# A two-stage FFT filter and gated feed-forward kernel: the operands of its f32r matmuls at other byte offsets

## The chip, the cores and the metric

The kernel runs on one core of a Trainium2 chip. The metric is the device time of one execution in microseconds, from its start to its end. "Before" has a median of 1559.99 us over 2 runs (1559.17 to 1560.82). A core has a matrix engine (TensorE; PE in the profile, and PEld for its weight loads), a vector engine (VectorE, DVE), a scalar engine (ScalarE, ACT), GpSimd (POOL) and DMA queues, of which SP issues most. Engines work on SBUF, 128 partitions with a run of bytes each, and TensorE writes its sums to PSUM. An *offset* in this document is where a tile's or a slice's first byte lies within its partition; only its remainder after division by 256 is spoken of.

## The reference

Eight batches of 3136 rows of 256 values are filtered along the rows in the frequency domain, and the result goes through a gated feed-forward layer of width 1024 whose gate is a three-tap convolution along the rows:

```python
X = np.fft.rfft(x, axis=1)
Y = X * (filt_r + 1j * filt_i)[None, :, :]
y = np.fft.irfft(Y, n=x.shape[1], axis=1).astype(np.float32)
h = np.maximum(y @ w_in, 0.0)                     # 3136 x 1024 per batch
hp = pad(h, 1 row of zeros at both ends)
conv_out = sum(conv_w[k] * hp[:, k:k + S, :] for k in range(3))
gate = 1.0 / (1.0 + np.exp(-conv_out))
out = (h * gate @ w_out).astype(np.float32)
```

## The kernel before

**Stage one** (up to about 360 us) does the filter. Each batch goes through 14 pieces: a first transform (`first`, L323), transposes (`turn`, L334), a second transform (`second`, L346 and L349), the product with the filter on VectorE and GpSimd (`filt`), and a third transform (`third`, L233), whose result is stored to `b_dram`. Its matmuls are plain float32, and each takes two passes over its columns in the trace (the transposes one). Beside it, `convert_weights` turns the 64-bit weights into float32 and splits each into a high and a low part of type f32r: `hi_act` (ScalarE, L146) writes the high part, rounded to f32r, and `lo_pool` (GpSimd, L152) the difference. These are the tiles `wi` (`w_in`: 2 halves of the contraction, k, by 1024 columns) and `wo` (`w_out`: 8 slices f by 256 columns).

**Stage two** is the feed-forward layer. The order of the work is written out by hand in the loop over m at the end: 28 chunks j of 896 rows, by 8 slices f of 128 hidden units, by 2 halves i of 448 rows. In each step TensorE does three things.

- `inner` (L456) makes a 128 x 450 block of hidden values from `wi` and the filtered rows `y`. Since both are split in two, a product is three matmuls, high by high, high by low and low by high (`mm3`, L177, L178, L179), for each of the two halves k: six matmuls of 450 columns, with a slice of `wi` as the stationary operand (the weights that are loaded) and 450 columns of `y` as the moving one.
- `project` (L488) multiplies the gated values `g` of an earlier step (6 steps behind, PLAG) with `wo`: three matmuls again for each block of 128 rows (L498 to L500), nine or twelve in a step, with `g` stationary and 256 columns of `wo` moving.
- in some steps `last_stage` (L215) does a part of the last transform of a later batch, from rows `br` that SP loads from `b_dram` (`last_load`, L198); `last_out` splits its result into `y` high (L146) and `y` low (L149).

ScalarE and VectorE work on the hidden block between: ReLU (L465), the three taps (L467, L472, L473), the sigmoid (L477), the product (L478); `split_g` then writes `g` high (ScalarE, L146) and `g` low (GpSimd, L152).

TensorE loads the weights of the next matmul while the moving rows of the present one stream in, so it reads two places of SBUF at once. Where tiles lie is set by the pools: `wc` holds `wi` and `wo` for the whole run, `y_even` and `y_odd` hold `y` of even and odd batches, `wp` holds four pairs of `g` in turn. The tiles' sizes therefore fix every offset:

```python
wi = [wc.tile([128, KT, FF], F32R, name=f"wi{h}") for h in range(2)]          # L189
wo = [wc.tile([128, NF, D], F32R, name=f"wo{h}") for h in range(2)]           # L190
ys[b] = [yps[b % 2].tile([128, KT, S + 2], F32R, name=f"y{h}") for h in range(2)]   # L203
gs[j, f] = [wp.tile([128, 2 * SUB], F32R, name=f"g{h}", bufs=4) for h in range(2)]  # L483
```

In the built program these come out, modulo 256 bytes, as follows: every slice of `wi` and `wo`, high and low, at 160; `g`, high and low, at 224; `y` high at 160 and `y` low at 192 in its first half (k = 0), 168 and 200 in its second, for each of the seven sub-blocks of 448 rows (1792 bytes, a multiple of 256) and in both pools.

Of the kernel before, what the change touches and what calls it, by code (L numbers as in the profile page):

```python
# [10 lines left out]
F32R = mybir.dt.float32r  # L11
# [5 lines left out]
S = 3136  # L17
# [3 lines left out]
D = 256  # L21
FF = 1024
KT = D // 128
NF = FF // 128
SUB = 448
# [99 lines left out]
def tile_fft_filter_gated_ffn(  # L125
# [16 lines left out]
    nc = tc.nc  # L142
    B = x.shape[0]

    def hi_act(dst, src):
        nc.scalar.activation(dst, src, AF.Copy)  # L146
# [4 lines left out]
    def lo_pool(dst, src, hi):  # L151
        nc.gpsimd.tensor_tensor(out=dst, in0=src, in1=hi.bitcast(F32), op=ALU.subtract)  # L152

    def to_f32(dst, raw, e, m):


        v = nc.vector
        pairs = raw.rearrange("p (n t) -> p n t", t=2)
        low, high = pairs[:, :, 0].bitcast(U32), pairs[:, :, 1]
        v.tensor_scalar(e, high, 3, 0x3FFFFFF8, op0=ALU.logical_shift_left, op1=ALU.bitwise_and)  # L160
        yield
        v.tensor_scalar(m, high, 30, 30, op0=ALU.logical_shift_right, op1=ALU.logical_shift_left)
        yield
        v.tensor_tensor(out=e, in0=e, in1=m, op=ALU.bitwise_or)
        yield
        v.tensor_scalar(m, high, 27, 0xF, op0=ALU.logical_shift_right, op1=ALU.bitwise_and)
        yield
        v.scalar_tensor_tensor(out=dst, in0=m, scalar=7.0, in1=e.bitcast(F32), op0=ALU.is_ge, op1=ALU.mult)
        yield
        v.tensor_scalar(e, dst.bitcast(I32), 23, 23, op0=ALU.logical_shift_right, op1=ALU.logical_shift_left)  # L170
        yield
        v.scalar_tensor_tensor(out=e.bitcast(F32), in0=low, scalar=2.0**-52, in1=e.bitcast(F32), op0=ALU.mult, op1=ALU.mult)
        yield
        nc.gpsimd.tensor_tensor(out=dst, in0=dst, in1=e.bitcast(F32), op=ALU.add)

    def mm3(ps, wh, wl, rh, rl, start=True, stop=True, **kw):
        nc.tensor.matmul(ps, lhsT=wh, rhs=rh, start=start, stop=False, **kw)  # L177
        nc.tensor.matmul(ps, lhsT=wh, rhs=rl, start=False, stop=False, **kw)  # L178
        nc.tensor.matmul(ps, lhsT=wl, rhs=rh, start=False, stop=stop, **kw)  # L179
# [4 lines left out]
    wc = ctx.enter_context(tc.tile_pool(name="wc", bufs=1))  # L184
# [1 line left out]
    cw = wc.tile([128, 3, NF], F32, name="cw")  # L186
    nc.gpsimd.memset(cw[:, 0, 0:1], 0.0)
    nc.scalar.activation(cw[:, 0, 0:1], cw[:, 0, 0:1], AF.Sigmoid)
    wi = [wc.tile([128, KT, FF], F32R, name=f"wi{h}") for h in range(2)]  # L189
    wo = [wc.tile([128, NF, D], F32R, name=f"wo{h}") for h in range(2)]  # L190


    ys, yps = {}, []
# [6 lines left out]

    def y_slices(b, sl):
        if sl.start == 0:
            ys[b] = [yps[b % 2].tile([128, KT, S + 2], F32R, name=f"y{h}") for h in range(2)]  # L203
            for t in ys[b]:
                nc.gpsimd.memset(t[:, :, 0:1].bitcast(F32), 0.0)
                nc.gpsimd.memset(t[:, :, S + 1:S + 2].bitcast(F32), 0.0)
        return (t[:, :, 1:S + 1].rearrange("p k (a c) -> p k c a", c=N2)[:, :, sl] for t in ys[b])
# [10 lines left out]
    def last_out(b, c):  # L218
        yh, yl = y_slices(b, slice(c, c + 2))
        pv = lasts.pop((b, c))[:, 0:4 * N1].rearrange("p (k c a) -> p k c a", c=2, a=N1)  # L220
        hi_act(yh, pv)
        lo_dve(yl, pv, yh)
# [5 lines left out]
    parts = {}  # L228
# [16 lines left out]
    with (  # L245
# [36 lines left out]
        def load_weights(k):  # L282
            raws[k] = raw = cv.tile([128, 2, 512], I32, name="raw")
            for part, src in enumerate((w_in, w_out)):
                nc.sync.dma_start(out=raw[:, part], in_=src[:, 512 * k:512 * k + 512])
# [6 lines left out]
        def convert_weights():  # L292

            for k in range(8):
                raw = raws.pop(k)
                em = cv.tile([128, 2, 512], I32, name="em", bufs=1)
                ws = cv.tile([128, 2, 256], F32, name="ws")
                yield from to_f32(ws.rearrange("p t n -> p (t n)"), raw.rearrange("p t n -> p (t n)"), em[:, 0], em[:, 1])
                yield
                parts = [[t.rearrange("p a b -> p (a b)")[:, 256 * k:256 * k + 256] for t in w] for w in (wi, wo)]  # L300
                for part, (wh, wl) in enumerate(parts):
                    hi_act(wh, ws[:, part])
                yield
                for part, (wh, wl) in enumerate(parts):
                    lo_pool(wl, ws[:, part], wh)
                yield
                if k < 6:
                    load_weights(k + 2)
# [130 lines left out]
    wp = ctx.enter_context(tc.tile_pool(name="wp", bufs=2, reuse_waits="tile"))  # L439
# [4 lines left out]
    hs, ts, gs, pos = {}, {}, {}, {}  # L444
# [8 lines left out]

    def inner(j, f, i):
        ps = ps_h.tile([128, 512], F32, name="ps_h")[:, 0:SUB + 2]
        fs = slice(128 * f, 128 * f + 128)  # L456
        b, u = divmod(2 * j + i, NSUB)
        us = slice(u * SUB, u * SUB + SUB + 2)
        for k in range(KT):
            mm3(ps, wi[0][:, k, fs], wi[1][:, k, fs], ys[b][0][:, k, us], ys[b][1][:, k, us], start=k == 0, stop=k == KT - 1)  # L460
        hs[j, f, i] = ps

    def relu(j, f, i):
# [16 lines left out]
    def split_g(j, f, i):  # L480
        t = ts.pop((j, f, i))
        if i == 0:
            gs[j, f] = [wp.tile([128, 2 * SUB], F32R, name=f"g{h}", bufs=4) for h in range(2)]  # L483
        gh, gl = (g[:, i * SUB:i * SUB + SUB] for g in gs[j, f])
        hi_act(gh, t)
        lo_pool(gl, t, gh)

    def project(j, f, i):  # L488
        gh, gl = gs[j, f]
        if f == 0 and i == 0:  # L490
            pos[j] = [ps_o.tile([128, 512], F32, name=f"po{k}") for k in range(4)], wp.tile([128, NT, D], F32, name="ot")
        po, ot = pos[j]
        tiles = range(4) if i == 0 else range(4, NT)
        for t in tiles:
            o = po[t // 2][:, t % 2 * D:t % 2 * D + D]
            sl = slice(128 * t, 128 * t + 128)
            first, last = f == 0 and t % 2 == 0, f == NF - 1
            nc.tensor.matmul(o, lhsT=gh[:, sl], rhs=wo[0][:, f], start=first, stop=False, skip_group_check=True)  # L498
            nc.tensor.matmul(o, lhsT=gh[:, sl], rhs=wo[1][:, f], start=False, stop=False, skip_group_check=True)  # L499
            nc.tensor.matmul(o, lhsT=gl[:, sl], rhs=wo[0][:, f], start=False, stop=last, skip_group_check=True)  # L500

    def evacuate(j, f, i):
        if f < NF - 1:
# [17 lines left out]
    for b in range(1, B):  # L521
        start = ((NSUB * (b - 1) - 1) // 2 + 1) * 16 + (4 if b == 1 else 0)
        stop = NSUB * b // 2 * 16 + NSUB * b % 2
# [73 lines left out]
```

## Time and profile before

| what | us |
|---|---|
| median of 2 runs | 1559.99 |
| the profiled execution's own time | 1559.94 |
| its span in the profile | 1558.2 |
| TensorE matmuls busy | 1537.8 |
| TensorE weight loads busy | 1418.2 |
| VectorE busy | 1297.0 |
| ScalarE busy | 1245.0 |
| GpSimd busy | 703.0 |

The span is the time between the first and the last recorded instruction; the 1.7 us between it and the execution's time lie around it. Busy time of an engine is the time in which at least one of its instructions was running. A matmul's recorded duration includes its way through the array, and the next starts before it ends; how fast matmuls follow each other is read from their starts. The profile's chain of waits goes back from the last instruction to whatever released each; its shares say which work the end hung on.

### The profile page before, as it was taken

Reading aid. Unit: us, or ns where it says so; the run is one execution under the profiler, and the core shown is the slowest. Engines: PE = TensorE matmul, PEld = TensorE weight load, DVE = VectorE, ACT = ScalarE, POOL = GpSimd, SP = SyncE. Lnnn points to the kernel's source line nnn. Section 1 sums busy time; section 2 is a strip of 40 time slices with the busy share of each in tenths; the row PEclk is TensorE's granted clock in tenths of the full one; section 3 lists DMA queues with packets and bytes.
Section 4 is the critical chain, followed back from the end, with each engine's and each line's share of the span. In section 5 each row is a group of like instructions: output and inputs, shape, how many; then the busy total and the mean of one; then the engine's idle time right before and its main releaser. Section 6 shows DMA issues by size and latency. Waiting matters only on the chain.

```text
span 1558.2 us, 27801 instructions
## 1 busy us (share of the span) xinstructions
PE 1537.8 (99%) x10320; PEld 1418.2 (91%) x10320; DVE 1297.0 (83%) x1978; ACT 1245.0 (80%) x2274; POOL 703.0 (45%) x625
## 2 busy tenths in 40 slices
PE   8999999998999999999999999999999999999998
PEld 7787778877999999999999999999999999999998
DVE  3888888788888888888888888888888888888887
ACT  5655555566888888888888888888888888888887
POOL 3455555533444444444444444444444434444444
PEclk9999999999999999999999999999999999999999
DMA  9855555452111011111111011111011110100001
GB/s 236 261 179 168 172 169 164 137 148 78 33 52 48 31 47 48 49 49 47 48 42 36 27 53 52 44 48 48 31 48 42 49 54 27 46 25 25 24 25 48
DMA packets 89062, 115.24 MB, mean 74 GB/s; under 512 B 7400, under 2 KB 60168, under 8 KB 88928
## 3 DMA queue, kind: packets, MB, share of 16 engines
q1 hardware_dynamic: 74592, 87.77, 18.4%
q10 hardware_dynamic: 14336, 25.70, 5.8%
q8 instruction: 82, 1.34, 0.4%
q14 instruction: 52, 0.43, 0.1%
HBM read 62.06 MB, written 51.38 MB: 73 GB/s over the span
## 4 chain that ended last, share of the span: by engine, by line
PE 94%; DMA 2%; DVE 1%; ACT 1%; issue 0%; SPq 0%; POOL 0%; ACTq 0%; POOLq 0%; DVEq 0%
PE ps_h L178 12%; PE ps_h L179 12%; PE ps_h L177 11%; PE po L498 11%; PE po L500 11%; PE po L499 11%; PE ps L233 6%; PE ps_h L215 5%; PE pp L346 5%; PE ps L323 5%; PE ps L334 3%; DMA x<-in_x 1%; PE ps L215 1%; DVE y L149 1%; ACT y L146 0%; PE pp L349 0%
## 5 line engine op out<-in xcount | busy, mean ns | idle before, releaser
L152 POOL TENSOR_TENSOR g<-t,g 128x448 fp32r<-128x448 f32 x448 | 517.1, 1154 | 663.5 <-ACT g L146 259.3
L498 PE MATMUL po<-wo,g 128*128 128x256 f32 x1568 | 441.4, 282 | 0.0
L500 PE MATMUL po<-wo,g 128*128 128x256 f32 x1568 | 433.9, 277 | 0.4 <-POOL g L152 0.4
L499 PE MATMUL po<-wo,g 128*128 128x256 f32 x1568 | 433.4, 276 | 0.0
L472 DVE SCALAR_TENSOR_TENSOR t<-ps_h,cw,t 128x448 f32<-128x448 f32 x448 | 305.7, 682 | 85.6 <-ACT t L467 75.2
L178 PE MATMUL ps_h<-y,wi 128*128 128x450 f32 x896 | 330.3, 369 | 5.6 <-DVE y L149 5.6
L177 PE MATMUL ps_h<-y,wi 128*128 128x450 f32 x896 | 329.1, 367 | 3.3 <-DVE t L478 1.9
L179 PE MATMUL ps_h<-y,wi 128*128 128x450 f32 x896 | 328.8, 367 | 0.0
L473 DVE SCALAR_TENSOR_TENSOR t<-ps_h,cw,t 128x448 f32<-128x448 f32 x448 | 306.5, 684 | 16.0
L467 ACT ACTIVATE t<-ps_h,cw 128x448 f32<-128x448 f32 x448 | 284.8, 636 | 43.2 <-ACT ps_h L465 2.6
L498 PEld LDWEIGHTS po<-wo,g 128*128 128x128 f32 x1568 | 294.8, 188 | 7.1
L499 PEld LDWEIGHTS po<-wo,g 128*128 128x128 f32 x1568 | 294.3, 188 | 5.7
L500 PEld LDWEIGHTS po<-wo,g 128*128 128x128 f32 x1568 | 294.5, 188 | 0.6 <-POOL g L152 0.6
L465 ACT ACTIVATE ps_h<-ps_h 128x450 f32<-128x450 f32 x448 | 251.8, 562 | 32.9 <-PE ps_h L179 27.0
L478 DVE TENSOR_TENSOR t<-ps_h,t 128x448 f32<-128x448 f32 x448 | 275.3, 615 | 0.1
L477 ACT ACTIVATE t<-t 128x448 f32<-128x448 f32 x448 | 255.0, 569 | 12.4 <-DVE t L473 11.2
L146 ACT ACTIVATE g<-t 128x448 fp32r<-128x448 f32 x448 | 254.7, 568 | 0.2 <-DVE t L478 0.2
L362 POOL TENSOR_TENSOR z<-u,v 120x512 f32<-120x512 f32 x112 | 156.6, 1398 | 184.3 <-DVE v L360 154.1
L178 PEld LDWEIGHTS ps_h<-y,wi 128*128 128x128 f32 x896 | 168.3, 188 | 14.7 <-DVE y L149 7.9
L179 PEld LDWEIGHTS ps_h<-y,wi 128*128 128x128 f32 x896 | 168.3, 188 | 13.9
L177 PEld LDWEIGHTS ps_h<-y,wi 128*128 128x128 f32 x896 | 169.9, 190 | 11.7 <-DVE t L478 2.9
L149 DVE TENSOR_TENSOR y<-ps_h,y 128x448 fp32r<-128x448 f32 x98 | 103.1, 1053 | 75.3 <-ACT y L146 75.3
(62 smaller groups left out, 1661.6 us busy)
## 6 DMA issues: line engine op xcount, KB each, us to landing
x<-in_x SPq DMA_DIRECT2D x112, 224.0 KB, 2.9
b_dram<-sb ACTq DMA_DIRECT2D x112, 224.0 KB, 2.3
br<-b_dram SPq DMA_DIRECT2D x112, 224.0 KB, 2.6
out<-ot SPq DMA_DIRECT2D x27, 896.0 KB, 4.1
raw<-in_w_in SPq DMA_DIRECT2D x8, 256.0 KB
raw<-in_w_out SPq DMA_DIRECT2D x8, 256.0 KB
t_sb<-in_fr SPq DMA_DIRECT2D x15, 112.0 KB
t_sb<-in_fi SPq DMA_DIRECT2D x14, 112.0 KB
```

What stands on the lines that cost most here:

```text
L152: nc.gpsimd.tensor_tensor(out=dst, in0=src, in1=hi.bitcast(F32), op=ALU.subtract)
L177: nc.tensor.matmul(ps, lhsT=wh, rhs=rh, start=start, stop=False, **kw)
L178: nc.tensor.matmul(ps, lhsT=wh, rhs=rl, start=False, stop=False, **kw)
L179: nc.tensor.matmul(ps, lhsT=wl, rhs=rh, start=False, stop=stop, **kw)
L467: nc.scalar.activation(t, h[:, 1:SUB + 1], AF.Copy, scale=cw[:, 1, f:f + 1])
L472: nc.vector.scalar_tensor_tensor(out=t, in0=h[:, 0:SUB], scalar=cw[:, 0, f:f + 1], in1=t, op0=ALU.mult, op1=ALU.add)
L473: nc.vector.scalar_tensor_tensor(out=t, in0=h[:, 2:SUB + 2], scalar=cw[:, 2, f:f + 1], in1=t, op0=ALU.mult, op1=ALU.add)
L477: nc.scalar.activation(t, t, AF.Sigmoid)
L478: nc.vector.tensor_mul(t, h[:, 1:SUB + 1], t)
L498: nc.tensor.matmul(o, lhsT=gh[:, sl], rhs=wo[0][:, f], start=first, stop=False, skip_group_check=True)
L499: nc.tensor.matmul(o, lhsT=gh[:, sl], rhs=wo[1][:, f], start=False, stop=False, skip_group_check=True)
L500: nc.tensor.matmul(o, lhsT=gl[:, sl], rhs=wo[0][:, f], start=False, stop=last, skip_group_check=True)
```

## The change

The tiles get larger, and their parts are taken from other places in them; what is computed, and in which order on the compute engines, stays.

- `wi` has, for each half k and slice f, 136 columns of room of which 128 are used, so that slice f starts 32 bytes further (modulo 256) than slice f - 1. `wo` has 264 columns of room for each slice, of which 256 are used: 32 bytes further per slice too. The conversion of the weights writes and reads the same values in that layout; for `wi` its 256 elements are now two pieces of 128.
- `y` has S + 64 columns of room, a multiple of 256 bytes for each half, and batch b starts 8 b columns, 32 b bytes, into it.
- `g` has 64 columns more, and chunk j starts 8 (j mod 8) columns, 32 (j mod 8) bytes, into it.

All tiles of a pair now have sizes that are multiples of 256 bytes, so that high and low parts start at equal offsets: in the built program `wi` and `wo` at 160 + 32 f, `y` at 160 + 32 b (odd batches) or 224 + 32 b (even ones) in both halves, `g` at 160 + 32 (j mod 8).

```diff
@@ -186,8 +186,8 @@
     cw = wc.tile([128, 3, NF], F32, name="cw")
     nc.gpsimd.memset(cw[:, 0, 0:1], 0.0)
     nc.scalar.activation(cw[:, 0, 0:1], cw[:, 0, 0:1], AF.Sigmoid)
-    wi = [wc.tile([128, KT, FF], F32R, name=f"wi{h}") for h in range(2)]
-    wo = [wc.tile([128, NF, D], F32R, name=f"wo{h}") for h in range(2)]
+    wi = [wc.tile([128, KT, NF, 136], F32R, name=f"wi{h}") for h in range(2)]
+    wo = [wc.tile([128, NF, D + 8], F32R, name=f"wo{h}") for h in range(2)]
 
 
     ys, yps = {}, []
@@ -200,7 +200,8 @@
 
     def y_slices(b, sl):
         if sl.start == 0:
-            ys[b] = [yps[b % 2].tile([128, KT, S + 2], F32R, name=f"y{h}") for h in range(2)]
+            ys[b] = [yps[b % 2].tile([128, KT, S + 64], F32R, name=f"y{h}") for h in range(2)]
+            ys[b] = [t[:, :, 8 * b:8 * b + S + 2] for t in ys[b]]
             for t in ys[b]:
                 nc.gpsimd.memset(t[:, :, 0:1].bitcast(F32), 0.0)
                 nc.gpsimd.memset(t[:, :, S + 1:S + 2].bitcast(F32), 0.0)
@@ -297,12 +298,14 @@
                 ws = cv.tile([128, 2, 256], F32, name="ws")
                 yield from to_f32(ws.rearrange("p t n -> p (t n)"), raw.rearrange("p t n -> p (t n)"), em[:, 0], em[:, 1])
                 yield
-                parts = [[t.rearrange("p a b -> p (a b)")[:, 256 * k:256 * k + 256] for t in w] for w in (wi, wo)]
-                for part, (wh, wl) in enumerate(parts):
-                    hi_act(wh, ws[:, part])
+                f = k % 4 * 2
+                parts = [[t[:, k // 4, f:f + 2, 0:128] for t in wi], [t[:, k, 0:D] for t in wo]]
+                values = [ws[:, 0].rearrange("p (f n) -> p f n", f=2), ws[:, 1]]
+                for (wh, wl), v in zip(parts, values):
+                    hi_act(wh, v)
                 yield
-                for part, (wh, wl) in enumerate(parts):
-                    lo_pool(wl, ws[:, part], wh)
+                for (wh, wl), v in zip(parts, values):
+                    lo_pool(wl, v, wh)
                 yield
                 if k < 6:
                     load_weights(k + 2)
@@ -453,11 +456,10 @@
 
     def inner(j, f, i):
         ps = ps_h.tile([128, 512], F32, name="ps_h")[:, 0:SUB + 2]
-        fs = slice(128 * f, 128 * f + 128)
         b, u = divmod(2 * j + i, NSUB)
         us = slice(u * SUB, u * SUB + SUB + 2)
         for k in range(KT):
-            mm3(ps, wi[0][:, k, fs], wi[1][:, k, fs], ys[b][0][:, k, us], ys[b][1][:, k, us], start=k == 0, stop=k == KT - 1)
+            mm3(ps, wi[0][:, k, f, 0:128], wi[1][:, k, f, 0:128], ys[b][0][:, k, us], ys[b][1][:, k, us], start=k == 0, stop=k == KT - 1)
         hs[j, f, i] = ps
 
     def relu(j, f, i):
@@ -480,7 +482,8 @@
     def split_g(j, f, i):
         t = ts.pop((j, f, i))
         if i == 0:
-            gs[j, f] = [wp.tile([128, 2 * SUB], F32R, name=f"g{h}", bufs=4) for h in range(2)]
+            gs[j, f] = [wp.tile([128, 2 * SUB + 64], F32R, name=f"g{h}", bufs=4) for h in range(2)]
+            gs[j, f] = [g[:, j % 8 * 8:j % 8 * 8 + 2 * SUB] for g in gs[j, f]]
         gh, gl = (g[:, i * SUB:i * SUB + SUB] for g in gs[j, f])
         hi_act(gh, t)
         lo_pool(gl, t, gh)
@@ -495,9 +498,9 @@
             o = po[t // 2][:, t % 2 * D:t % 2 * D + D]
             sl = slice(128 * t, 128 * t + 128)
             first, last = f == 0 and t % 2 == 0, f == NF - 1
-            nc.tensor.matmul(o, lhsT=gh[:, sl], rhs=wo[0][:, f], start=first, stop=False, skip_group_check=True)
-            nc.tensor.matmul(o, lhsT=gh[:, sl], rhs=wo[1][:, f], start=False, stop=False, skip_group_check=True)
-            nc.tensor.matmul(o, lhsT=gl[:, sl], rhs=wo[0][:, f], start=False, stop=last, skip_group_check=True)
+            nc.tensor.matmul(o, lhsT=gh[:, sl], rhs=wo[0][:, f, 0:D], start=first, stop=False, skip_group_check=True)
+            nc.tensor.matmul(o, lhsT=gh[:, sl], rhs=wo[1][:, f, 0:D], start=False, stop=False, skip_group_check=True)
+            nc.tensor.matmul(o, lhsT=gl[:, sl], rhs=wo[0][:, f, 0:D], start=False, stop=last, skip_group_check=True)
 
     def evacuate(j, f, i):
         if f < NF - 1:
```

On SP's queue two of the first four loads of `br` wait for more than before, since the pool `lp` now begins 960 bytes lower and its buffers lie on other tiles of stage one (`Pool_49`, `DVE_49` and `PE_49` are the counters of those engines, the `DMAHW` ones those of DMA queues). Before, where stage one's last loads of `x` end and stage two's first loads of `br` begin:

```order
L314 DMA x<-in_x 112x512 [waits DMAHW5_49,PE_49]
L198 DMA br<-b_dram_57 112x2x256 [waits DMAHW5_49,Pool_49]
L198 DMA br<-b_dram_57 112x2x256 [waits DMAHW6_49,PE_49]
L198 DMA br<-b_dram_57 112x2x256 [waits DMAHW0_49]
L198 DMA br<-b_dram_57 112x2x256 [waits DMAHW1_49]
```

The same place after, with the lines of the changed file:

```order
L317 DMA x<-in_x 112x512 [waits DMAHW5_49,PE_49]
L198 DMA br<-b_dram_57 112x2x256 [waits DMAHW5_49,DMAHW6_49,DVE_49,Pool_49]
L198 DMA br<-b_dram_57 112x2x256 [waits DMAHW6_49,PE_49]
L198 DMA br<-b_dram_57 112x2x256 [waits DMAHW0_49,Pool_49]
L198 DMA br<-b_dram_57 112x2x256 [waits DMAHW1_49]
```

No load moved; the first waits for VectorE and another DMA queue too, the third for GpSimd.

## The prediction

> **What bounds the kernel now.** I read the page first, for the engine that the span belongs to; then the table by windows, for the stage in which the change acts; then the groups by line, for the two kinds of matmul that the change touches; and last the timeline, for how far apart these matmuls start, which their durations do not tell.
>
> ```profile
> span 1558.2 us, 27801 instructions
> PE 1537.8 (99%) x10320; PEld 1418.2 (91%) x10320; DVE 1297.0 (83%) x1978; ACT 1245.0 (80%) x2274; POOL 703.0 (45%) x625
> PE 94%; DMA 2%; DVE 1%; ACT 1%; issue 0%; SPq 0%; POOL 0%; ACTq 0%; POOLq 0%; DVEq 0%
> PE ps_h L178 12%; PE ps_h L179 12%; PE ps_h L177 11%; PE po L498 11%; PE po L500 11%; PE po L499 11%; PE ps L233 6%; PE ps_h L215 5%; PE pp L346 5%; PE ps L323 5%; PE ps L334 3%; DMA x<-in_x 1%; PE ps L215 1%; DVE y L149 1%; ACT y L146 0%; PE pp L349 0%
> ```
>
> TensorE is busy 99% of the span and is 94% of the chain that ended last; 68 points are the six lines of the feed-forward stage (L177 to L179, L498 to L500). The six are what the change moves in memory.
>
> ```profile
> core 0: us, PE busy (x) PEld busy (x) DVE busy (x) ACT busy (x) POOL busy (x), PEclk, DMA share, GB/s
> 600.00:900.00 300.00, 298.82 (x2087) 287.10 (x2086) 256.71 (x396) 259.54 (x479) 130.36 (x122) 1.00 0.14 44
> 900.00:1200.00 300.00, 298.82 (x2088) 287.08 (x2087) 255.90 (x394) 260.13 (x479) 129.96 (x121) 1.00 0.14 44
> ```
>
> In the steady part of that stage matmuls cover 298.8 of 300 us and weight loads 287.1. ScalarE (260 us) and VectorE (256 us) have some 40 us of 300 free, 13%; GpSimd has more than half. The clock is granted in full. So only the rate of matmul after matmul counts here, until it rises by 13%.
>
> ```profile
> L498 PE MATMUL po<-wo,g 128*128 128x256 f32 x1568 | 441.4, 282 | 0.0
> L499 PE MATMUL po<-wo,g 128*128 128x256 f32 x1568 | 433.4, 276 | 0.0
> L177 PE MATMUL ps_h<-y,wi 128*128 128x450 f32 x896 | 329.1, 367 | 3.3 <-DVE t L478 1.9 <-ACT y L146 1.2
> L498 PEld LDWEIGHTS po<-wo,g 128*128 128x128 f32 x1568 | 294.8, 188 | 7.1
> ```
>
> These durations (367 and 276 ns) overlap; what a matmul costs is the distance from its start to the next start. One step of the loop, six inner matmuls and twelve projections:
>
> ```profile
> 903.49 0.37 PE L177 MATMUL ps_h<-y,wi 128*128 128x450 f32 x1
> 903.70 0.36 PE L178 MATMUL ps_h<-y,wi 128*128 128x450 f32 x1
> 903.90 0.37 PE L179 MATMUL ps_h<-y,wi 128*128 128x450 f32 x1
> 904.11 0.36 PE L177 MATMUL ps_h<-y,wi 128*128 128x450 f32 x1
> 904.31 0.37 PE L178 MATMUL ps_h<-y,wi 128*128 128x450 f32 x1
> 904.51 0.36 PE L179 MATMUL ps_h<-y,wi 128*128 128x450 f32 x1
> 904.72 0.28 PE L498 MATMUL po<-wo,g 128*128 128x256 f32 x1
> ...
> 905.97 0.28 PE L500 MATMUL po<-wo,g 128*128 128x256 f32 x1
> 906.08 0.37 PE L177 MATMUL ps_h<-y,wi 128*128 128x450 f32 x1
> ```
>
> From 903.49 to 904.72 six inner matmuls take 1.23 us, 205 ns each; from 904.72 to 906.08 twelve projections take 1.36 us, 113.3 ns each. Over the kernel that is 3 x 896 = 2688 x 205 ns = 551 us and 3 x 1568 = 4704 x 113.3 ns = 533 us: 1084 us, 70% of the time, whose rate is all that the change can alter.
>
> **The change part by part.** Instructions: none is added, removed or moved on the compute engines; every matmul keeps its shape and its place in the order. Term: 0.
>
> Two loads of `br` on SP's queue get further waits, because the larger tiles shift the pool of `br` over tiles of the weight conversion. What they wait for is the conversion's last readers and writers.
>
> ```profile
> L152 POOL TENSOR_TENSOR wi<-ws,wi x8: 720/730/742, 112.1 to 301.2; 128x256 fp32r<-128x256 f32 x8
> L198 SPq DMA_DIRECT2D br<-b_dram x13: 304/305/305, 331.7 to 395.0; - x13
> ```
>
> The conversion's last subtraction starts at 301.2 us and takes 0.7; the first of these loads is issued at 331.7. The new waits are over 30 us before they are asked. Behind them on SP stand only further `br` loads, and nobody waits longer for those. Term: 0, hidden by 30 us.
>
> The conversion writes `wi` through a two-piece pattern instead of one flat piece, with the same 256 elements: 8 x 0.41 us on ScalarE and 8 x 0.73 us on GpSimd, off TensorE's path in a stage in which both have room. Were each 10% longer it would be under 1 us, hidden. Term: 0.
>
> The offsets themselves. Before, the built program has, modulo 256 bytes, `wi` and `wo` at 160 for every slice, `g` high and low both at 224, `y` high at 160 and low at 192, and the second half (k = 1) of `y` 8 bytes further, 168 and 200. After it, high and low agree everywhere, all starts are multiples of 32, and slice against batch (inner) and slice against chunk (projection) run through all eight distances. So each pair of streams that TensorE reads at once (the moving rows of one matmul, the weights of the next) meets at all eight distances about equally often.
>
> Does the distance matter in the trace? The nearest rows are the inner matmuls, which already differ in it:
>
> ```profile
> L177 PE MATMUL ps_h<-y,wi x896: 363/367/579, 365.1 to 1545.1; 128*128 128x450 f32 x180
> L178 PE MATMUL ps_h<-y,wi x896: 365/369/579, 367.3 to 1545.3; 128*128 128x450 f32 x180
> L179 PE MATMUL ps_h<-y,wi x896: 360/367/579, 367.6 to 1545.5; 128*128 128x450 f32 x180
> ```
>
> L177 and L178 have the same weights and differ in the moving tile alone, high or low part, 32 bytes apart. Across lines and halves the durations mostly lie from 363 to 369 ns, and the starts above show the same: 0.21, 0.20, 0.21, 0.20, 0.20, 0.21. In that step the k = 0 half (all starts multiples of 32) takes 903.49 to 904.11 = 0.62 us, the k = 1 half (all 8 bytes off) 0.61. So aligned or not, the three sum to the same; a single transition shifts by about 3 ns to either side, and neighbours cancel it. In the projections, whose high and low weights already agree, the step is as even as it can be read. I therefore take 0 ns for the mean of either kind, as the value nearest to these rows.
>
> Its bounds. On the good side: the float32 matmuls of the first stage show what a pass costs when nothing holds it up.
>
> ```profile
> 337.75 0.87 PE ps L233 x4
> 338.61 0.86 PE pp L346 x2
> 600.87 0.88 PE ps_h L215 x8
> ```
>
> L233's passes of 256 columns take 0.87/4 = 217 ns, L346's of 512 columns 430 ns: 0.83 ns a column and 4 ns fixed. The f32r matmuls run at about half of that a column (205/450 = 0.455), and an unhindered one would, at 0.416, take 191 ns for 450 columns and 110.5 for 256 (an estimate from these rows). L215, whose 112 columns are short against its weight load, is no quicker than 0.88/8 = 110. Relief of everything would be 2688 x 14 + 4704 x 2.8 = 38 + 13 = 51 us, down to 1509.
>
> On the bad side:
>
> ```profile
> L215 PEld LDWEIGHTS ps_h<-m_sb,br 112*128 112x128 f32 x224 | 29.3, 191 | 1.1
> ```
>
> If all inner matmuls went like the slowest kind, 3 ns above the middle of 363 to 369, that is 2688 x 3 = 8 us. The slowest regular weight load of this width takes 191 ns where the projection's takes 188; with loads busy 96% of the time, 3 ns more on each would be passed on: 4704 x 3 = 14 us. Together 22 us, up to 1582.
>
> Here a rule of the Trainium skill speaks against the change. Its page "SBUF — State Buffer", section "Who interferes with whom", gives TensorE two read ports of its own, one for moving rows and one for weights, independent of each other, and says that TensorE never waits on anyone: by it no offset matters and the sum stays at 0. The evenness of the rows above agrees; what it leaves unexplained is why an inner matmul takes 205 ns and not some 190.
>
> Sum: 0 + 0 + 0 + 0, against the profiled execution's own time, 1559.94 us, of which 1558.2 are the span. The median of the runs is 1559.99, the same. The likeliest time is 1560 us.
>
> **The rivals.** *Relief.* The 14 ns that an inner matmul takes beyond the estimate of 191 come from its moving rows and the next weights being fetched from the same place in the 256-byte pattern; now most pairs lie apart. For it: the excess is there, and before all inner pairs but the last of each six lie within 40 bytes (160, 168, 192 or 200 against 160). Against it: the pair that lies apart, the last inner matmul (168) before a projection (`g`, 224), is spaced 904.72 - 904.51 = 0.21, no shorter; and the projections, 64 bytes apart, have 113.3 against a floor of 110 that their weight loads set. All of it would give 1509; if the excess goes for half of the distances, 1560 - 19 - 6 = 1535. Faster by over 2% (31 us, about what a measurement of this kernel can tell from no change) begins where about 12 of the 14 ns go, or six tenths of the whole 51 us.
>
> By the page "TensorE: Matmul & The Clock Gate", section "Back-to-back issue gap", a matmul of N columns follows the last after N/2.4 + 2.5 ns: 190 for 450 and 109 for 256, so that the kernel would stand near 1500 if the offsets were all that keeps it from this. This trace's 205 and 113 do not agree with it, and no run here yet shows why.
>
> *Slower: the weight loads pay.* `g` is the stationary operand of the projections and now begins at eight different offsets, of which before only one (224) was in use; likewise `wi`. If some of these eight lengthen a load, TensorE waits for it at once, since loads fill 287 of 300 us and a projection (113 ns) is bound by its load. For it: that tight cover. Against it: L177's and L215's loads, at other offsets (160), take 188 to 191 as well. With 3 ns on each projection it gives 1574; it is slower by over 2% from 6.6 ns per projection on (31/4704), which is eight offsets of which one costs 50 ns or all cost 6.6.
>
> *No change because nothing changes.* The loads of weights or the writes of `y` and `g` could take up odd offsets at a price on ScalarE or GpSimd, but these have 40 and 170 us of 300 free: 1560 again, part of the forecast.
>
> **How the numbers follow.** No systematic effect, 1550 to 1570: 0.65, and the likeliest, at 1560. Relief of part, under 2%, 1529 to 1550: 0.13; relief of most, below 1529: 0.08. Slower within 2%, 1570 to 1591: 0.09; beyond: 0.05. So faster 0.08, same 0.87, slower 0.05. The range reaches from 1534 to 1576: it leaves out 0.08 and about 0.03 of the partial relief below, and 0.05 and about 0.03 above, 0.19 in all, and takes in the half-relief at 1535 and the 3 ns on projections at 1574.
>
> **What would show it.** Right: starts 205 ns apart on average in the inner matmuls and 113 in the projections, with a pattern by slice and batch that averages out; PE still near 299 of 300 us in the steady windows, and the first stage unchanged to the microsecond (first inner matmul at 365.1). The `br` loads still begin near 331.7 if the new waits are free. Relief shows as the inner matmuls' durations falling towards 350 and their chain pieces to 0.19; if TensorE's busy share drops while ScalarE's rises past 90%, the relief was real and more. The slower rival shows as weight loads above 190 ns for some chunks and slices and not for others. I would be wrong if the spread of 363 to 369 is not all that offsets can do: distances from 64 to 160 bytes between moving rows and weights do not occur in the inner matmuls before, and the trace cannot speak for them.

## The result and the profile after

The changed kernel takes 1583.39 us (median of 2 runs, 1583.14 to 1583.63), 1.015 times the time before, with a 95% interval of 1.0106 to 1.0194. The forecast was 1560 us, 1534 to 1576. The kernel is slower, by less than 2%, and lies 7 us above the range.

The page of the changed kernel: its span, its busy times, and the chain that ended last, by line. The lines have moved: L501 to L503 are the projections (L498 to L500 before), L216 is the last transform (L215).

```profile
span 1581.8 us, 27803 instructions
PE 1559.7 (99%) x10320; PEld 1439.8 (91%) x10320; DVE 1296.5 (82%) x1978; ACT 1246.8 (79%) x2274; POOL 704.5 (45%) x625
PE 94%; DMA 2%; DVE 2%; ACT 1%; issue 0%; POOL 0%; SPq 0%; ACTq 0%; POOLq 0%; DVEq 0%
```

TensorE is as busy as before, 99%, with 22 us more of matmuls; VectorE, ScalarE and GpSimd have the same work as before to within 2 us. The windows of the steady part say the same the other way round:

```profile
600.00:900.00 300.00, 298.81 (x2051) 287.62 (x2051) 251.51 (x387) 256.19 (x471) 128.26 (x119) 1.00 0.14 44
```

In the same 300 us TensorE is covered as before (298.8) and the clock is granted in full, but it gets through 2051 matmuls where it got through 2087. It does not wait; it runs slower. The groups by line (busy us, mean ns of one) say which:

```profile
L501 PE MATMUL po<-wo,g 128*128 128x256 f32 x1568 | 448.0, 286 | 0.0
L502 PE MATMUL po<-wo,g 128*128 128x256 f32 x1568 | 439.8, 280 | 0.0
L177 PE MATMUL ps_h<-y,wi 128*128 128x450 f32 x896 | 330.3, 369 | 3.3 <-DVE t L480 1.8 <-ACT y L146 1.2
L501 PEld LDWEIGHTS po<-wo,g 128*128 128x128 f32 x1568 | 296.0, 189 | 5.5
```

A projection lasts 4 ns longer (286 and 280 against 282 and 276), an inner matmul 2 ns or nothing (369 against 367 on L177), a weight load 1 ns. What counts is the time from start to start. A block of projections from the timeline of the changed kernel, in which the moving rows of `wo` and the weights from `g` start at equal offsets (distance 0):

```profile
729.35 0.29 PE L501 MATMUL po<-wo,g 128*128 128x256 f32 x1
729.48 0.28 PE L502 MATMUL po<-wo,g 128*128 128x256 f32 x1
729.59 0.28 PE L503 MATMUL po<-wo,g 128*128 128x256 f32 x1
...
730.67 0.28 PE L503 MATMUL po<-wo,g 128*128 128x256 f32 x1
730.79 0.37 PE L177 MATMUL ps_h<-y,wi 128*128 128x450 f32 x1
```

Twelve projections take 730.79 - 729.35 = 1.44 us, 120 ns each, where before they took 1.36 us, 113.3 each. Summed over every start of the trace (for each matmul the time to the next matmul's start), the projections take 564.8 us instead of 543.9, the inner matmuls 561.6 instead of 561.8. The first inner matmul starts at 367.6 us instead of 365.1. The conversion of the weights already ends 2.6 us later than before (305.2 against 302.6 us); over the profiles of this study the start of the inner matmuls lies between 364.7 and 367.8, late and early with the same layout of `wi` and `wo`, so I count these 2.5 us as the spread of stage one. 20.9 - 0.2 + 2.5 = 23.2 of the 23.6 us by which the span grew.

In what follows the *distance* of a matmul is the offset of its moving rows less that of the weights loaded for the next one, modulo 256 bytes, from the built programs. The time of a matmul is that from its start to the next start; means are taken over the projections that another projection follows, and over inner matmuls, without those over 135 and 230 ns (98 projections, nearly all behind a part of the last transform, and some 30 inner matmuls in each run). In the changed kernel all eight distances occur, so its trace is an experiment of its own:

| distance, bytes | 0 | 32 | 64 | 96 | 128 | 160 | 192 | 224 |
|---|---|---|---|---|---|---|---|---|
| projection after projection, ns | 119.2 | 117.0 | 117.5 | 119.7 | 118.5 | 118.2 | 116.0 | 118.2 |
| inner matmul, ns | 203.8 | 204.8 | 204.1 | 205.8 | 205.0 | 204.5 | 205.6 | 205.0 |

Before, every projection that another one follows had the distance 192, and 113.6 ns on average. Sorted by the offset of `wo` alone, or of `g` alone, the same projections all have 118 ns: among these offsets, all multiples of 32, it is the distance that counts and not where either lies.

### The profile page after: what moved, and what is told of

The parts are those of the page before. It is cut to its first block, busy times and chain, and to the rows that moved or that the text cites. A ratio compares the mean times of both kernels' runs of the same rounds, so it can differ in the third digit from the quotient of the medians.

```text
span 1581.8 us, 27803 instructions
## 1 busy us (share of the span) xinstructions
PE 1559.7 (99%) x10320; PEld 1439.8 (91%) x10320; DVE 1296.5 (82%) x1978; ACT 1246.8 (79%) x2274; POOL 704.5 (45%) x625
## 4 chain that ended last, share of the span: by engine, by line
PE 94%; DMA 2%; DVE 2%; ACT 1%; issue 0%; POOL 0%; SPq 0%; ACTq 0%; POOLq 0%; DVEq 0%
PE ps_h L178 12%; PE po L501 12%; PE po L502 11%; PE po L503 11%; PE ps_h L179 11%; PE ps_h L177 11%; PE ps L234 5%; PE ps_h L216 5%; PE ps L326 5%; PE pp L349 5%; PE ps L337 3%; DMA x<-in_x 1%; DMA t_sb<-in_fi 1%; PE ps L216 1%; DVE y L149 1%; ACT y L146 0%
## 5 line engine op out<-in xcount | busy, mean ns | idle before, releaser
L501 PE MATMUL po<-wo,g 128*128 128x256 f32 x1568 | 448.0, 286 | 0.0
L503 PE MATMUL po<-wo,g 128*128 128x256 f32 x1568 | 440.0, 281 | 0.4 <-POOL g L152 0.4
L502 PE MATMUL po<-wo,g 128*128 128x256 f32 x1568 | 439.8, 280 | 0.0
L177 PE MATMUL ps_h<-y,wi 128*128 128x450 f32 x896 | 330.3, 369 | 3.3 <-DVE t L480 1.8
L501 PEld LDWEIGHTS po<-wo,g 128*128 128x128 f32 x1568 | 296.0, 189 | 5.5
L503 PEld LDWEIGHTS po<-wo,g 128*128 128x128 f32 x1568 | 295.3, 188 | 0.6 <-POOL g L152 0.6
L177 PEld LDWEIGHTS ps_h<-y,wi 128*128 128x128 f32 x896 | 169.2, 189 | 12.7 <-DVE t L480 2.8
```

The lines of the kernel that those rows point to most:

```text
L501: nc.tensor.matmul(o, lhsT=gh[:, sl], rhs=wo[0][:, f, 0:D], start=first, stop=False, skip_group_check=True)
L502: nc.tensor.matmul(o, lhsT=gh[:, sl], rhs=wo[1][:, f, 0:D], start=False, stop=False, skip_group_check=True)
L503: nc.tensor.matmul(o, lhsT=gl[:, sl], rhs=wo[0][:, f, 0:D], start=False, stop=last, skip_group_check=True)
```

## The experiments

Three theories stood at the beginning. Theory A: the distance sets the rate of projections. Theory B: the larger strides of the tiles do, such as the 8448 instead of 8192 bytes between the high and low part of `wo`. Theory C: the inner matmuls' new offsets leave TensorE's reads in a state that slows the projections after them. All experiments but the two scans and the two at the end ran in rounds with the kernel before on the same chip; ratios are to it, with 95% intervals. Each is told as a difference to the kernel named.

**Only `g` moves.** From the kernel before:

```diff
-gs[j, f] = [wp.tile([128, 2 * SUB], F32R, name=f"g{h}", bufs=4) for h in range(2)]
+gs[j, f] = [wp.tile([128, 2 * SUB + 64], F32R, name=f"g{h}", bufs=4) for h in range(2)]
+o = j % 8 * 8
+gs[j, f] = [g[:, o:o + 2 * SUB] for g in gs[j, f]]
```

> Only the gated values start 32 bytes further per chunk; wi, wo and y lie as before. Theory A (the distance modulo 256 between the moving rows of a projection and the weights loaded for the next one sets how fast projections follow each other; before it stood at 192, a good one, and now it runs through all eight): projections go from 113.3 to 117-119 ns between starts, inner matmuls stay at 205 ns, 1577 to 1583 us. Theory B (the tiles' larger strides, high and low 8448 instead of 8192 bytes apart in wo, disturb the reads): wo is unchanged here, so 1558 to 1563 us. Theory C (the inner matmuls' new offsets leave TensorE's reads in a bad state for the projections): 1558 to 1563 us.

**Only `wo` moves.** From the kernel before:

```diff
-wo = [wc.tile([128, NF, D], F32R, name=f"wo{h}") for h in range(2)]
+wo = [wc.tile([128, NF, D + 8], F32R, name=f"wo{h}") for h in range(2)]
```

> Only wo's slices start 32 bytes further each; wi, y and g lie as before. Theory A: the same eight distances come up, by slice instead of by chunk: projections 117-119 ns, 1577 to 1583 us, and not more for both shifts together than for one. Theory B: also slower, 1577 to 1583. Theory C: 1558 to 1563 us.

They took 1580.9 us (1.0119, 1.0104 to 1.0135) and 1580.6 us (1.0120, 1.0105 to 1.0135), with projections at 117.7 and 117.8 ns and inner matmuls at 205.0 and 204.6. Either shift alone gives nearly all that both give together, as A has it. `wi` and `y` lie as before in both, so C alone cannot be the cause, and `wo` lies as before in the first, so its strides cannot be either. Split by distance, 192 is alone in keeping 113.7 and 113.9 ns; the others lie from 117.1 to 119.8. The rows of the second are those of the changed kernel but for 1 ns:

```profile
L503 PE MATMUL po<-wo,g 128*128 128x256 f32 x1568 | 446.9, 285 | 0.0
L504 PE MATMUL po<-wo,g 128*128 128x256 f32 x1568 | 439.8, 280 | 0.0
```

**Only the inner matmuls' tiles move; the projections stay at 192.** From the changed kernel:

```diff
-wo = [wc.tile([128, NF, D + 8], F32R, name=f"wo{h}") for h in range(2)]
+wo = [wc.tile([128, NF, D], F32R, name=f"wo{h}") for h in range(2)]
-gs[j, f] = [g[:, j % 8 * 8:j % 8 * 8 + 2 * SUB] for g in gs[j, f]]
+o = 16
+gs[j, f] = [g[:, o:o + 2 * SUB] for g in gs[j, f]]
```

> wi and y as in the changed kernel, with all eight distances in the inner matmuls; wo as before and g at a fixed offset that keeps the projections' distance at 192. Theory A: projections 113-114 ns, inner 205 ns, 1556 to 1566 us. Theory B: 1558 to 1563. Theory C: projections at 116-119 ns although their own distance did not change, 1572 to 1583 us.

**Equal offsets without steps.** From the changed kernel, with `g` as just shown (inner distance 0, projections 192):

```diff
-wi = [wc.tile([128, KT, NF, 136], F32R, name=f"wi{h}") for h in range(2)]
-wo = [wc.tile([128, NF, D + 8], F32R, name=f"wo{h}") for h in range(2)]
+wi = [wc.tile([128, KT, NF, 128], F32R, name=f"wi{h}") for h in range(2)]
+wo = [wc.tile([128, NF, D + 64], F32R, name=f"wo{h}") for h in range(2)]
-ys[b] = [t[:, :, 8 * b:8 * b + S + 2] for t in ys[b]]
+o = 0 if b % 2 else 48
+ys[b] = [t[:, :, o:o + S + 2] for t in ys[b]]
```

> High and low parts at equal offsets and the larger strides of wo (1280 bytes per slice), y and g, but no step per slice, batch or chunk: the inner distance is 0 and the projections' 192 throughout. Theory A: projections 113.3 ns, inner 203-206 ns, 1553 to 1564 us. Theory B: strides alone are enough, 1574 to 1584 us. Theory C: no statement beyond the inner matmuls, 1555 to 1565.

1570.8 us (1.0058, 1.0041 to 1.0074), with projections at 115.6 ns, and 1568.9 us (1.0044, 1.0029 to 1.0059), with 115.7. Both lie outside the ranges of all three theories, A's included: they keep the distance at 192 and still have nearly half of the projections' loss (2.0 and 2.2 of 4.5 ns). The timeline of the second shows where. A block of nine that follows inner matmuls:

```profile
700.00 0.28 PE L503 MATMUL po<-wo,g 128*128 128x256 f32 x1
700.12 0.28 PE L504 MATMUL po<-wo,g 128*128 128x256 f32 x1
700.24 0.28 PE L505 MATMUL po<-wo,g 128*128 128x256 f32 x1
700.36 0.28 PE L503 MATMUL po<-wo,g 128*128 128x256 f32 x1
700.48 0.28 PE L504 MATMUL po<-wo,g 128*128 128x256 f32 x1
700.59 0.28 PE L505 MATMUL po<-wo,g 128*128 128x256 f32 x1
700.70 0.28 PE L503 MATMUL po<-wo,g 128*128 128x256 f32 x1
```

The first four starts are 0.12 us apart, the later ones 0.11 to 0.12. In single nanoseconds, the most frequent course of a block of twelve between inner matmuls (161 such blocks in each trace; all but one, which holds a wait, have sums within 1 ns of each other):

```
kernel before          112 114 113 113 114 113 113 114 113 113 114 113   mean sum 1359
equal without steps    122 118 119 116 114 113 114 113 113 114 113 113   mean sum 1383
```

So the rate settles at 113.3 ns, that of the distance 192, but the beginning is lost: 24 ns per block. The changed kernel at the distance 192 shows more: some blocks settle at 113.3, others stay at 117 to 118 to the end (116 119 117 119 117 118 118 117 118 118 118 121). One distance has two rates, so something else than the distance decides which. B (for the strides of `g` and of `wo` here) and C are both still possible for this part.

**The distance 0 throughout, all else as in the last one.** From it:

```diff
-o = 16
+o = 0
 gs[j, f] = [g[:, o:o + 2 * SUB] for g in gs[j, f]]
```

> As the experiment with all offsets fixed (inner distance 0, projections 192, which took 1568.9 us with projections 115.7 ns apart), but g starts 64 bytes lower, so that the projections' distance is 0 throughout. Theory A (the distance sets the rate of projections): distance 0 took 119.2 ns in the changed kernel, so 119-120 ns here, 4704 x 3.6 = 17 us more, 1583 to 1590 us. Rival C (only the state that the inner matmuls leave counts, and that is the same): 115-116 ns, 1566 to 1572 us.

1586.3 us (1.0170, 1.0151 to 1.0188), projections at 119.6 ns, blocks 118 120 120 120 ... to the end (sum 1438). One edit of 64 bytes makes the projections 18.8 us longer in the sum of their starts (571.7 against 552.9 us; the two times, from two chips, differ by 17). The edit also moves the distance from the last inner matmul to the first `g`, from 192 to 0, but the 120 ns last to the end of the block, and no block of the runs above settles there at the distance 192: it is the projections' own distance, as A has it. In the rows:

```profile
L503 PE MATMUL po<-wo,g 128*128 128x256 f32 x1568 | 451.0, 288 | 0.0
L504 PE MATMUL po<-wo,g 128*128 128x256 f32 x1568 | 443.1, 283 | 0.0
```

**Other inner distances, projections at 192.** From the experiment with equal offsets, 160 and then 64:

```diff
-o = 0 if b % 2 else 48
+o = 40 if b % 2 else 24
```

> As the experiment with all offsets fixed, projections at 192, but y starts so that the inner distance is 160 instead of 0. In the changed kernel a projection block at 192 that followed inner matmuls at 160 always fell into the faster of its two rates (113.5 ns), and inner matmuls at 160 sometimes ran at 200 ns. Theory A+C (distance, and the state left by the matmuls before): projections 113.3-114.5 ns, inner 200-206 ns, 1545 to 1566 us. Theory A alone (the state does not matter, 192 gave 115.7): projections 115-116 ns again, 1565 to 1573 us.

```diff
-o = 0 if b % 2 else 48
+o = 16 if b % 2 else 0
```

> The same with the inner distance at 64, after which the changed kernel's projection blocks at 192 were now in the slow, now in the fast rate, and at which inner matmuls sometimes ran at 200 ns. Theory A+C: projections 113-116 ns, inner 200-206 ns, 1545 to 1572 us. Theory A alone: projections 115-116 ns, 1560 to 1573 us.

1576.4 us (1.0107, 1.0087 to 1.0128), projections 115.9 and inner 206.9 ns; 1574.1 us (1.0092, 1.0076 to 1.0109), 115.7 and 206.0. Both lie above all expected ranges, and the gain was a miss: the quick inner matmuls (200 ns) and clean starts seen at these distances in the changed kernel did not come back at fixed offsets. The inner matmuls got slower by 2.2 and 1.3 ns than in the kernel before, and the time with them.

The second of the two shows something more. All its blocks lie at the same offsets, and so do the six inner matmuls before each, yet the first eight projections of a block take either about 907 or about 943 ns, and some blocks of twelve run at 113.3 ns, others at 117.8 throughout (sums 1360 and 1414). The two take turns: of 249 blocks that follow another one with nothing but six inner matmuls between, 248 are slow after a quick one or quick after a slow one. So a state passes from block to block through the six inner matmuls.

**`g` in steps of 8 bytes.** As the first experiment, with

```diff
-o = j % 8 * 8
+o = 2 * j
```

> The layout before with g alone shifted, by 8 bytes per chunk: 28 distances of the projections in steps of 8 bytes. Theory A: the spacing of projections varies with the distance between 113 and 120 ns, with 113.5 at and near 192, mean 116-119 ns, 1572 to 1584 us; whether steps of 8 bytes make a difference from 32 is open. Theory C: 113-114 ns at all distances, since the inner matmuls are those of before, 1558 to 1564 us.

1583.2 us (one run), in A's range. Of 28 distances, two are good: 192 with 113.8 ns and 88 with 113.5. 168 has 115.9: its blocks begin slowly and then settle at 113.3 too. All others lie from 117.1 to 121.2, 184 among them with 118.2, where A expected 113.5 near 192. Both neighbours of 88 and of 168, 8 bytes away, are slow, and so is 184; 200 was not among the 28.

**The strides alone, with `wi` and `y` exactly as before.** From the experiment with equal offsets:

```diff
-ys[b] = [yps[b % 2].tile([128, KT, S + 64], F32R, name=f"y{h}") for h in range(2)]
-o = 0 if b % 2 else 48
+ys[b] = [yps[b % 2].tile([128, KT, S + 2], F32R, name=f"y{h}") for h in range(2)]
+o = 0
 ys[b] = [t[:, :, o:o + S + 2] for t in ys[b]]
-o = 16
+o = 0
 gs[j, f] = [g[:, o:o + 2 * SUB] for g in gs[j, f]]
```

> The larger strides of wo (1280 bytes per slice) and g, at fixed offsets that keep the projections' distance at 192, with wi and y exactly as before (low part of y 32 bytes from the high one, second half 8 bytes further). Theory A+C (the distance, and the state in which the inner matmuls leave TensorE's reads; strides that are multiples of 256 bytes do not matter): the first projection of a block at once at the steady spacing, projections 113.5 ns, inner 204.7 ns, 1557 to 1564 us, no different from before. Theory B (strides): 1566 us or more, as with y and wi at equal offsets, where it took 1568.9.

1560.7 us against 1560.6 (1.0002, 0.9993 to 1.0011), projections at 113.6, inner at 204.7, and the blocks begin at once with 113. The rows are those of the kernel before:

```profile
span 1557.6 us, 27803 instructions
L503 PE MATMUL po<-wo,g 128*128 128x256 f32 x1568 | 441.4, 281 | 0.0
L504 PE MATMUL po<-wo,g 128*128 128x256 f32 x1568 | 433.4, 276 | 0.0
```

B falls here too: slices of `wo` 1280 bytes apart and `g` of 3840 bytes cost nothing. And since in the built programs only `y` lies elsewhere, modulo 256, than in the experiment with equal offsets (`g` comes out at 224 in both), C is shown for the other part: the start of a projection block hangs on the offsets of `y` in the inner matmuls before it.

**Inner distances in steps of 8 bytes.** From the kernel before: slices of `wi` 130 columns apart in rows of FF + 64, `y` in tiles of S + 66 columns with

```diff
+o = b % 4 * 16
+ys[b] = [t[:, :, o:o + S + 2] for t in ys[b]]
```

> Projections at 192 and wo, g as before; the inner distance runs through 32 values in steps of 8 bytes (slices of wi 8 bytes further each, batches of y 64 bytes), with the low part of y 32 bytes from the high one and the second half 8 bytes further, as before. Theory A+C: six inner matmuls take between 1210 and 1245 ns depending on the distance, the value of before (1227.5) being near the middle, and projections are 113.5 to 116 ns depending on what the inner matmuls before leave: 1558 to 1574 us. If the inner matmuls know a narrow good distance as projections do at 192, some value lies clearly below 1210 ns. Theory A alone: projections 113.5 to 114 throughout.

1571.5 us (one run). Of the 32 distances none is clearly good for the inner matmuls: six take 1222 to 1244 ns, against 1227.5 before. The projections (115.7 ns on average) begin without loss after a few of them only. Added up over six inner matmuls and eight projections, no distance beats the kernel before: distance 0, which is its own layout, has its sum to within 1 ns, then come 160 and 152, 3 and 5 ns above it.

**Which part of `y` keeps the start clean?** Theory D: the distance of the last inner matmul to the first `g` alone. Theory E: the whole pattern of the six. Two layouts between that of before and that with equal offsets: first high and low equal and the second half 8 bytes further; then low 32 bytes from high, both halves equal. The first from the strides-alone, the second from the equal-offsets experiment:

```diff
-ys[b] = [yps[b % 2].tile([128, KT, S + 2], F32R, name=f"y{h}") for h in range(2)]
-o = 0
-ys[b] = [t[:, :, o:o + S + 2] for t in ys[b]]
+ys[b] = [yps[b % 2].tile([128, KT, S + 66], F32R, name=f"y{h}") for h in range(2)]
+o = 64
+ys[b] = [t[:, :, o - 8 * h:o - 8 * h + S + 2] for h, t in enumerate(ys[b])]
```

> As the experiment that gave back the time of before, but high and low parts of y at equal offsets; the second half of y stays 8 bytes further. The last inner matmul before a projection block keeps its distance of 200 to the first g. Theory D (the last inner distance alone decides in which state the projections begin): projections 113.5 ns, 1556 to 1563 us. Theory E (the whole pattern of the six inner matmuls decides): projections at 114.5 to 116 ns, 1564 to 1572 us.

```diff
-ys[b] = [t[:, :, o:o + S + 2] for t in ys[b]]
+ys[b] = [t[:, :, o + 8 * h:o + 8 * h + S + 2] for h, t in enumerate(ys[b])]
```

> The other half of it: the low part of y 32 bytes from the high one as before, but both halves k at equal offsets, so that the last inner distance to g is 192 as in the experiment with all offsets fixed. Theory D: projections 115.7 ns as there, 1566 to 1571 us. Theory E: anything between 113.5 and 116 ns, and not bound to the result of the run beside it.

1570.3 us (1.0062, 1.0047 to 1.0077): projections 115.0, inner 206.3. 1565.1 us (1.0026, 1.0016 to 1.0035): projections 115.6, inner 203.1. The first keeps the last distance before a block, 200, and still begins with 124 116 114: D falls, though the second by itself would fit its 115.7 ns. Neither part of the offsets of `y` is enough. E is what is left of the two, but it is not the whole: at the inner distance 64 the same six inner matmuls had quick and slow blocks behind them in turn. The second has the quickest inner matmuls of all runs at fixed offsets, 1.6 ns under those of before (4 us), and gives 9 us back at the starts.

**The seam alone.** With that quicker inner pattern, `wo` and `g` move together per slice, so that the projections stay at 192, in steps of 32 and of 8 bytes. Shown for 8, of one matmul its moving operand alone; the conversion writes `wo` in the same steps. In the first expectation the unit is a cycle of 0.83 ns: its 136 are the 113.3 ns of a projection, its 1473 the 1227.5 ns of the six inner matmuls before.

```diff
-rhs=wo[0][:, f, 0:D]
+rhs=wo[0][:, f, 2 * f:2 * f + D]
-o = 16
+o = (16 + 2 * f) % 64
```

> The inner matmuls of the experiment with y's low part 32 bytes further (1461 of 1473 cycles, but projections at 115.6 ns); wo and g move together, 32 bytes further per slice f, so that the projections' distance stays 192 while the distances at the two seams (last inner matmul to first g, last projection to first wi) run through all eight. Theory E (the projections' slow starts come from how the six inner matmuls before leave the two streams, and the seam is part of that): blocks of some f start at once at 136 cycles, others lose 20 to 45 cycles, 1558 to 1570 us. If seams do not matter: all blocks like those of that experiment, 115.6 ns, 1563 to 1567 us.

> The same with wo and g moving together 8 bytes further per slice f. Theory E: again a start that depends on f, and with steps of 8 bytes too, 1558 to 1570 us. If seams do not matter: all blocks alike, 1563 to 1567 us.

1566.9 and 1577.8 us (one run each), projections 115.8 and 117.7 ns. The first time fits both ranges; what speaks for E is that blocks differ by slice. With steps of 32 bytes the first eight projections take from 906 to 947 ns on average, the shortest where the distance from the last inner matmul to `g` is 64. Where the distance from the last projection to `wi` is 96 as well, the inner six take 1225 ns, so that the sum is 3 ns under that of before; this was not built by itself. The second run lies above the 1558 to 1570 that E gave it: every slice whose offset is an odd multiple of 8 bytes settles at 120 ns, at the distance 192.

No version beat the kernel before.

## Why the prediction was wrong, point by point

- *What bounds the kernel*: right. TensorE is the bound, nothing waits, and only the spacing of starts changed.
- *Instructions, `br` loads, conversion, 0 each*: right in the sum, and for the loads by luck. The 331.7 us of the first load came from a window that began at 330; in the whole trace the first `br` load of the kernel before is issued at 302.7 us, as the conversion's last subtraction ends (302.6), for which SP's queue had waited 3.0 us. There was no slack of 30 us. The first load after the change is issued at 302.4 us, the second at 320.7 instead of 318.1, where the conversion is as late already; in neither trace does an engine wait for one of these loads.
- *The mean of the inner matmuls, 0 ns*: right, 204.8 against 204.7 ns, for an even mix of distances. It does not hold for each layout: at fixed offsets the mean went from 203.1 to 206.9 ns.
- *The mean of the projections, 0 ns*: this is the step that failed. It measured +4.5 ns (118.05 against 113.56), 20.9 us. The prediction took it from "the nearest rows", those of the inner matmuls, which show several distances, and read the evenness of the projections as a sign that offsets do not matter. But all projections had one distance, and rows that hold one value cannot say what another does. It was one of three distances among 28 at which projections settle at 113.3 ns, and a change that runs through eight leaves it in seven cases of eight.
- *The bound on the bad side, 3 ns a projection*: too small, and from the wrong mechanism. It came from the longest weight load, and the recorded loads lengthened by 1 ns on average (189 against 188), by 3 ns in the experiment with distance 0 throughout (191). What lengthens is the spacing: in that experiment by 6 ns, to 119.6. That the two bad-side terms add up to 1582 us, 1 us from the result, is luck: 8 of their 22 us were for inner matmuls, which gave none.
- *The slower rival, 1574 at 3 ns on each projection*: the right sign and place, with the size short by a third (14 of 20.9 us). Its mechanism, that some of the eight offsets of `g` lengthen a load, is not borne out: in the changed kernel the loads average 188.5 to 188.7 ns at each of the eight.
- *Relief*: wrong for both kinds. Distances from 64 to 160, which the trace before could not speak for, give projections of 117.5 to 119.7 ns and inner matmuls of 204.1 to 205.8.
- *The rule of the Trainium skill weighed against the change* ("SBUF — State Buffer", section "Who interferes with whom": TensorE's two read ports are independent, and it never waits on anyone): what the prediction took from it, that no offset matters, does not hold for this kernel's f32r matmuls. Moving `g` by 64 bytes against `wo` made the projections 18.8 us longer. Whether the two ports themselves disturb each other no run here shows.
- *The rule on the spacing* ("TensorE: Matmul & The Clock Gate", section "Back-to-back issue gap", of the Trainium skill): the section calls N/2.4 + 2.5 ns the gap of a matmul by itself and gives other spacings for a stream of weight loads and matmuls, which this kernel is, so the 1500 us did not follow from it. No layout here came near 190 or 109 ns: the quickest means of a run are 203.1 and 113.6.

What stays open is the mechanism inside. In six traces with one layout throughout the courses repeat to 1 ns, and in a seventh they alternate in order, while the other engines work beside them; this speaks against interference from other engines, without ruling it out. Whether the two streams meet in SBUF or later no run here can tell. Nor is it known why a block begins clean after one pattern of inner matmuls and not after another, or how the state passes from block to block.

## What to carry to other kernels

When matmuls follow each other as closely as weight loads allow, the byte distance between the moving rows and the next weights can be a parameter of the kernel: here 32 bytes more for each slice of `wo` cost 1.2%. So print the offsets of both operands beside the starts before and after any change of a tile's size. A trace in which all matmuls of a kind have one distance bounds nothing for other distances; one cheap run that steps a tile through them, one step for each pass of a loop, shows all of them at once. What such a scan shows for a value between changing neighbours need not hold when the value is fixed everywhere, so the candidate has to be run itself.

## What the runs showed of the hardware that was not expected

- Projections of 256 f32r columns with a new 128 x 128 weight each settle at 113.3 ns at distances of 192, 88 and 168 bytes (at 168 after a slow start, 115.9 on average), and take 117 to 121 ns on average at the 25 other distances tried in steps of 8; 8 bytes decide.
- At the distance 192 a run of such matmuls has two lasting rates, 113.3 and about 117.7 ns, and where it settles at 113.3 it can lose some 24 ns in its first matmuls. What comes before decides, and it reaches back past the six inner matmuls: at the inner distance 64, quick and slow blocks alternated in 248 of 249 pairs.
- At the distance 192, with `wo` and `g` moved together, starts at odd multiples of 8 bytes settle at 120 ns, at even ones at 113.3 or 117.7: the distance is not all.
- The courses are exact: in the kernel before and in five of the runs at fixed offsets the sum of twelve starts varies by 1 ns over 160 blocks of a trace, with ScalarE, VectorE and GpSimd at work beside them.
